# Splitting each tile's second products into two steps, laid between the steps of the next block's first products, in a Fourier-layer and mixture-of-experts kernel

## Chip, cores and metric

The kernel runs on one core of one Trainium2 chip. The metric is the device time of one execution in microseconds (us). The profile has its own execution, with a time and a span (first to last instruction) of its own.

## What is computed

The input is x, 8 batches of 2496 tokens by 256 features, in fp32. A Fourier layer comes first, a mixture of experts after it.

```python
X = rfft(x, axis=1)                       # per batch
Yr = Xr @ w_r - Xi @ w_i + b_r            # 256 x 256
Yi = Xr @ w_i + Xi @ w_r + b_i
Y  = soft_threshold(Yr, Yi, 0.01)
y  = irfft(Y)                             # 19968 tokens x 256
e  = argmax(y @ w_gate)                   # one of 8 experts per token
g  = softmax(y @ w_gate)[e] * sigmoid(y @ w_output_gate)[e]
out = g * (relu(y @ w1[e]) @ w2[e])       # w1: 256 x 1024, w2: 1024 x 256
```

## The kernel before

**Two parts.** The Fourier part works batch by batch: first transform, spectrum, soft threshold, inverse transform; it writes y to DRAM (`yd`). The expert part gathers tokens that are sorted by expert into 163 tiles of 128 tokens. The first 64 tiles hold tokens of the first four batches and are taken as 32 **pairs** (two tiles of one expert, m = 2); the other 99 are **singles** (m = 1), from all batches. A pair or a single is a **block**. The pairs begin while the last batch's inverse is still being computed.

**One block.** A token tile is gathered (`yg`, line 1236, on POOL), scaled and split into two fp16 parts (`yhl`, lines 1255 and 1256, on ACT and DVE) and transposed by a DMA from SP (`eT`, line 1269). The *first products* (`up`, line 1354) multiply it with the first half of the expert's weights, in steps: a single has 2 steps of 24 matmuls of 128 columns, a pair 4 steps of 12 matmuls of 256 columns. Every step has a PSUM bank of its own, which ACT (line 1364) and DVE (line 1365) then read: relu, and a split into two fp16 parts, into `hh`. The *second products* (`down`, line 1325) take 24 matmuls of 256 columns for each tile, from `hh` and the second half of the weights, into one bank. ACT scales the sum into `o` (line 1336), and POOL scatters it to DRAM by an indirect DMA (line 1339).

**Weights.** An expert has 2 MB, kept in DRAM (`wd`) and fetched by SP in two halves of 1 MB: the *up half* and the *down half* (`fetch`, line 1222). There are three buffers (`wbuf`), used in turn; the first four blocks have two of them. A block whose buffer already holds its expert skips its fetch on the device (`cond`). So a new expert costs six halves: two for each of the first three of its blocks. An up half may be loaded when the first products of the block three before (two before, for the first ones) have been read, a down half when that block's second products have.

**What sets the order.** The class `Issue` runs all stages as coroutines over modelled times and writes down each engine's instructions in the order that results; on the chip every engine keeps its order, and waits for semaphores. A request such as `yield "P", r, 2.61, f, True` asks for the engine (P is TensorE, A ACT, D DVE, G POOL, S SP) with a priority `r` (the smallest that is ready goes first), a modelled duration, and a PSUM bank if the last field is there. `r` grows by 5.6 from tile to tile. There are eight PSUM banks, two `hh` places for a pair (each becomes two for singles), three `eT` places for a pair (likewise six for singles) and five of `yhl`. The second products are asked for by `block` when all steps of `hh` have been written (`io.set("hh", t)`), with the priority r + 4m.

Of the kernel before, what the change touches and what calls it, by code (L numbers as in the profile page):

```python
# [15 lines left out]
AF = mybir.ActivationFunctionType  # L16
# [7 lines left out]
N = B * S  # L24
# [93 lines left out]
P = 69.05  # L118
# [21 lines left out]

EARLY = dict(yg=3, yhl=2, eT=1, hh=1, o=1)
PLACES = dict(yg=6, yhl=5, eT=3, hh=2, o=5)
KW = 4
YR, ZR, AN, WR, SR = 2, 3, 6, 3, 6
S1 = 5
# [34 lines left out]
class Issue:  # L180
# [64 lines left out]
    def give(self, slots, n=1):  # L245
        for _ in range(n):
            if slots.queue:
                self.go(slots.queue.pop(0))
            else:
                slots.n += 1  # L250
# [25 lines left out]
def tile_fft_moe(ctx, tc, x, w_r, w_i, b_r, b_i, w_gate, w_og, w1, w2, f1, f4, cmat, gmat, m16, out, dbg=None):  # L276
    nc = tc.nc
    V, A, G, T = nc.vector, nc.scalar, nc.gpsimd, nc.tensor
# [19 lines left out]
    def bank(i):  # L298
        return pps.tile([128, 512], F32, tag=f"ps{i}", name=f"ps{i}")
# [123 lines left out]
    io = Issue(list(range(8)))  # L423
# [4 lines left out]
    st = {}  # L428
# [567 lines left out]
    def plan(ph):  # L996
# [30 lines left out]
        if ph == 0:  # L1027
            route["fl"] = pc.tile([1, T_ALL], I32, name="flg")
            route["ei"] = pc.tile([1, T_ALL], I32, name="ebi")
            V.memset(route["fl"][:, 0:2 * KW + 1], 1)  # L1030
        V.tensor_copy(route["ei"][:, t0:t0 + n], ev[0:1])
        fl = lambda a, b, c, d, step: V.tensor_tensor(route["fl"][:, a:b], eb[0:1, a:b], eb[0:1, c:d:step], ALU.not_equal)
        if ph == 0:
            fl(4, 2 * KW, 0, 2 * KW - 4, 1)
            fl(2 * KW + 1, T_A, 2 * KW - 5, T_A - 6, 1)
        else:
# [38 lines left out]
    sidx = pc.tile([128, T_ALL], I32, name="sidx")  # L1075
# [110 lines left out]
    def open_h():  # L1186
# [5 lines left out]
        io.set("opened")  # L1192
        for k, n in PLACES.items():
            for i in range(EARLY[k], n):
                io.put(slots[k], i)

    def place(k, i, shape, dt):
        return pools["w" if i < EARLY[k] else "h"].tile(shape, dt, tag=f"{k}{i}", name=f"{k}{i}")

    def wplace(k):  # L1200
        return k % 2 if k < KW else (k - KW + 2) % 3

    def before(k):

        return None if k < 2 or k == KW else k - 2 if k < KW else k - 3

    def fetch(r):

        yield "w open"
        for k, (t, n) in enumerate(BLOCKS):  # L1210
            yield "plan", 0 if t < T_A else 1
            if k == KW:
                yield "opened"
# [63 lines left out]
    def part(k, i, shape):  # L1277

        if (k, i) not in parts_:
            parts_[k, i] = place(k, i, shape, F16)  # L1280
        return parts_[k, i]

    def back(k, t, i):

        if t >= T_A:
            io.put(slots[k + "1"], i)
            return
        st["n" + k] = st.get("n" + k, 0) + 1
        if st["n" + k] <= T_A // 2 - PLACES[k]:
            io.put(slots[k], i)  # L1290
        else:
            for h in range(2):
                io.put(slots[k + "1"], (i, h))

    def block(k, r):

        t, m = BLOCKS[k]
        for i in range(m):
            yield "eT", t + i
        ie, eT = st["eT", t]  # L1300
        yield "w", t, 0
        if m == 2:
            ih = yield slots["hh"]
            hh = part("hh", ih, [128, 4096])
        else:
            ih = yield slots["hh1"]
            hh = part("hh", ih[0], [128, 4096])[:, 2048 * ih[1]:2048 * (ih[1] + 1)]
        hh = hh.rearrange("p (v f n) -> p v f n", v=2, f=8)
        w = W[wplace(k)][:, :4096].rearrange("p (c h v f) -> p c h v f", c=2, h=2, v=2)
        st["nh", t], st["nu", t] = 0, 0  # L1310
        for half in range(2 * m):
            io.go(up(t, m, half, w, eT, ie, hh, r))
        yield "hh", t
        yield "w", t, 1
        w = W[wplace(k)][:, 4096:].rearrange("p (i v c d) -> p i v c d", i=4, v=2, c=2)
        for i in range(m):
            io.go(down(t + i, m, i, w, hh, ih, r + 4 * m))

    def down(t, m, n, w, hh, ih, r):
        def f(i):  # L1320
            pt = bank(i)
            k = 0
            for fc in range(8):
                for v, vw in ((0, 0), (0, 1), (1, 0)):
                    T.matmul(pt[:, :256], hh[:, v, fc, 128 * n:128 * n + 128], w[:, fc // 2, vw, fc % 2], start=(k == 0), stop=(k == 23))  # L1325
                    k += 1
            return pt

        i, pt = yield "P", r, 2.61, f, True
        if n == m - 1:  # L1330
            back("hh", t, ih)
            io.set("down", t - n)
        io_ = yield slots["o"]
        o = place("o", io_, [128, 256], F32)
        fac = st.pop(("fac", t))
        yield "A", r - 4, 0.47, lambda: A.activation(o, pt[:, :256], AF.Copy, scale=fac)  # L1336
        io.free(i)
        give("fac")
        yield "G", r - 4, 1.0, lambda: G.indirect_dma_start(out=out, out_offset=bass.IndirectOffsetOnAxis(ap=sidx[:, t:t + 1], axis=0), in_=o, in_offset=None, bounds_check=N - 1, oob_is_err=False)  # L1339
        yield 3.6  # L1340
        io.put(slots["o"], io_)

    def up(t, m, half, w, eT, ie, hh, r):

        c = 4 // m

        def f(i):
            pt = bank(i)
            for j in range(c):
                g = c * half + j  # L1350
                n = 0
                for dh in range(2):
                    for vw, v in ((0, 0), (0, 1), (1, 0)):
                        T.matmul(pt[:, 128 * m * j:128 * m * (j + 1)], w[:, dh, g // 4, vw, 128 * (g % 4):128 * (g % 4) + 128], eT[:, :m, v, dh], start=(n == 0), stop=(n == 5))  # L1354
                        n += 1
            return pt

        i, pt = yield "P", r, (1.34, 1.31)[m - 1], f, True
        st["nu", t] += 1
        if st["nu", t] == 2 * m:  # L1360
            back("eT", t, ie)
            io.set("up", t)
        hv = hh[:, :, c * half:c * half + c].rearrange("p v c n -> p v (c n)")
        yield "A", r, 0.6, lambda: A.activation(hv[:, 0], pt, AF.Relu)  # L1364
        yield "D", r, 0.69, lambda: V.scalar_tensor_tensor(hv[:, 1], pt, 0.0, hv[:, 0], ALU.max, ALU.subtract)  # L1365
        io.free(i)
        st["nh", t] += 1
        if st["nh", t] == 2 * m:
            io.set("hh", t)

    def blocks_(r):
        for k, (t, m) in enumerate(BLOCKS):
            yield "w open"
            io.go(block(k, r + 5.6 * t))
# [47 lines left out]
```

## Time and profile before

| | before |
|---|---|
| time, median of 3 runs | 1507.56 us (1501.02 to 1515.1) |
| profiled execution | 1500.14 us; span 1498.4 us |
| busy TensorE, matmuls / weight loads | 1420.1 / 1280.4 us (95% / 85%) |
| busy DVE, ACT, POOL | 970.0, 717.4, 590.9 us |
| mean granted TensorE clock | 0.983 |
| DMA | 285.33 MB, mean 190 GB/s |

Busy times are sums over an engine's instructions. Matmuls are pipelined and their ends are modelled, so how fast TensorE goes is read from the starts of its rows and from the gaps before them. A row of the timeline gives start, length, engine, line, operation, tiles and count; the brackets at its end hold the idle time before it and what ended it. The rows of waits give engine, line and what was waited for, then the sum in us, how often, and the longest. The rows of windows give for a stretch the busy time of each engine with instructions in brackets, the granted clock, the DMA share and GB/s.

### The profile page before, as it was taken

What the parts mean: (1) busy time and instruction counts of PE and PEld (TensorE: products, weight loads), DVE (VectorE), ACT (ScalarE), POOL (GpSimd) and SP (SyncE); (2) the same over time, 40 slices, a digit from 0 to 9 for tenths busy, and PEclk for the clock granted to TensorE, in tenths of its full rate; (3) what the DMA queues carried; (4) which work ended last, traced back from release to release, by engine and by line L of the source; (5) the groups of instructions that cost most, each with busy time, mean ns of one, the idle gap of its engine ahead of it and who ended that gap; (6) DMA issues with size and microseconds to landing.
All of it is one profiled execution on the core that took longest, in us unless ns stands there. A gap on an engine that the chain in (4) does not pass through costs nothing. (4 is left out here: it accounts for less than half of the span.)

```text
span 1498.4 us, 42257 instructions
## 1 busy us (share of the span) xinstructions
PE 1420.1 (95%) x16192; PEld 1280.4 (85%) x16192; DVE 970.0 (65%) x2911; ACT 717.4 (48%) x1386; POOL 590.9 (39%) x664
## 2 busy tenths in 40 slices
PE   4799999998989989999999999999999999999998
PEld 4689887887778867878999988999898989999997
DVE  3677777769988878677777685555454555454532
ACT  4666765767665746343333333433333333333432
POOL 0454535444455545334333324344243333433311
PEclk8799999999999999999999999999999999999999
DMA  8879999999989898988865788765938476477420
GB/s 227 198 164 212 217 225 198 218 221 214 215 209 209 205 223 202 208 241 231 239 185 147 213 227 218 220 208 123 233 80 234 106 208 220 98 235 212 102 51 20
DMA packets 329955, 285.33 MB, mean 190 GB/s; under 512 B 277702, under 2 KB 286536, under 8 KB 317721
## 3 DMA queue, kind: packets, MB, share of 16 engines
q1 hardware_dynamic: 313127, 239.40, 65.4%
q0 software_dynamic: 15648, 42.17, 10.5%
q8 instruction: 127, 2.08, 0.6%
q10 hardware_dynamic: 978, 1.06, 0.3%
q14 instruction: 75, 0.61, 0.1%
HBM read 337.41 MB, written 58.91 MB: 264 GB/s over the span
## 5 line engine op out<-in xcount | busy, mean ns | idle before, releaser
L1354 PE MATMUL ps<-eT,wbuf 128*128 128x128 f16 (+1 forms) x6288 | 451.9, 232 | 5.6 <-DMA wbuf<-wd 4.3
L1325 PE MATMUL ps<-wbuf,hh 128*128 128x256 f16 x3912 | 444.8, 273 | 8.9 <-DVE hh L1365 4.0
L1354 PEld LDWEIGHTS <-wbuf 128*128 128x128 f16 x6288 | 419.7, 98 | 26.0 <-DMA wbuf<-wd 5.2
L1325 PEld LDWEIGHTS <-hh 128*128 128x128 f16 x3912 | 379.5, 98 | 57.0 <-DVE hh L1365 6.5
L1339 POOL DMA_INDIRECT out<-o,sidx x163 | 167.4, 1027 | 494.0 <-ACT o L1336 270.7
L1365 DVE SCALAR_TENSOR_TENSOR hh<-ps,hh 128x512 f16<-128x512 f32 x326 | 220.3, 689 | 206.7 <-ACT hh L1364 195.3
L1364 ACT ACTIVATE hh<-ps 128x512 f16<-128x512 f32 x326 | 188.3, 596 | 194.1 <-PE ps L1354 176.7
L670 PE MATMUL ps<-whl,xt 128*128 128x256 f16 x1920 | 229.3, 276 | 3.8 <-ACT xt L655 1.7
L670 PEld LDWEIGHTS <-xt 128*128 128x128 f16 x1920 | 190.2, 99 | 40.8 <-ACT xt L655 2.5
L1236 POOL DMA_INDIRECT yg<-yd,gidx x163 | 161.2, 989 | 93.2 <-DVE p2e L366 35.4
L1256 DVE SCALAR_TENSOR_TENSOR yhl<-yg,ys,yhl 128x256 f16<-128x256 f32 x163 | 79.6, 488 | 145.1 <-ACT yhl L1255 135.6
L1336 ACT ACTIVATE o<-ps,fac 128x256 f32<-128x256 f32 x163 | 76.8, 471 | 200.0 <-PE ps L1325 168.4
L1255 ACT ACTIVATE yhl<-yg,ys 128x256 f16<-128x256 f32 x163 | 82.2, 505 | 160.6 <-DMA eT<-yhl 78.1
L588 PE MATMUL ps<-f1t,x 117*128 117x120 f32 (+1 forms) x704 | 91.3, 291 | 6.1 <-issue 4.9
L588 PEld LDWEIGHTS ps<-f1t,x 117*128 117x128 f32 (+1 forms) x704 | 88.7, 207 | 7.4 <-issue 5.0
L689 POOL CAST zhl<-z 128x512 f16<-128x512 f32 x44 | 28.4, 647 | 139.1 <-DVE z L686 70.8
L765 PE MATMUL ps<-bdt,f4t 120*117 120x512 f16 x264 | 70.4, 390 | 10.5 <-ACT ste L716 8.5
L700 PE MATMUL ps<-gt,zhl 128*128 128x128 f16 x960 | 65.3, 220 | 9.9 <-DVE zhl L690 3.9
L700 PEld LDWEIGHTS <-zhl 128*128 128x128 f16 x960 | 58.1, 98 | 17.4 <-DVE zhl L690 4.4
L597 ACT ACTIVATE at<-ps,sx 128x480 f16<-128x480 f32 (+1 forms) x88 | 55.3, 649 | 34.2 <-PE ps L588 31.5
L685 ACT ACTIVATE zhl<-ps,sc 128x512 f32<-128x512 f32 x80 | 54.7, 687 | 32.9 <-PE ps L670 28.2
L690 POOL TENSOR_TENSOR zhl<-z,zhl 128x512 f16<-128x512 f32 x51 | 60.6, 1188 | 24.8 <-ACT zhl L688 21.4
(187 smaller groups left out, 1610.5 us busy)
## 6 DMA issues: line engine op xcount, KB each, us to landing
wbuf<-wd SPq DMA_DIRECT2D x262, 1024.0 KB
yd<-yt SPq DMA_DIRECT2D x120, 158.4 KB
x<-in_x SPq DMA_DIRECT2D x120, 156.0 KB
wr<-in_moe_w SPq DMA_DIRECT2D x32, 512.0 KB
wd<-wsp SPq DMA_DIRECT2D x64, 256.0 KB
yg<-yd,gidx POOLq DMA_INDIRECT x163
eT<-yhl SPq DMA_TRANSPOSE x163
out<-o,sidx POOLq DMA_INDIRECT x163
```

Source lines behind the costliest of these rows:

```text
L588: T.matmul(pv[:, dh, :, m * j:m * j + m], xs[:k, j0 + j, 128 * dh:128 * dh + 128], fw, start=True, stop=True)
L670: T.matmul(yp[:, 256 * j:256 * j + 256], xt_[:, v, 2 * dh + j, 64 - 64 * u:192 - 64 * u], whl[:, dh, vw, 256 * u:256 * u + 256], start=Fal ...
L700: T.matmul(bv[:, j], zhl[:, vz, c:c + 128], gt[:, 2 * p + j, v], start=(n == 0), stop=(n == 2))
L1236: yield "G", r + 5.6 * t - 30, 1.0, lambda: G.indirect_dma_start(out=yg, out_offset=None, in_=src, in_offset=bass.IndirectOffsetOnAxis(ap= ...
L1255: yield "A", r - 10, 0.5, lambda: A.activation(yhl[:, 0], yg[:, :256], AF.Copy, scale=s)
L1256: yield "D", r - 10, 0.48, lambda: V.scalar_tensor_tensor(yhl[:, 1], yg[:, :256], s, yhl[:, 0], ALU.mult, ALU.subtract)
L1325: T.matmul(pt[:, :256], hh[:, v, fc, 128 * n:128 * n + 128], w[:, fc // 2, vw, fc % 2], start=(k == 0), stop=(k == 23))
L1336: yield "A", r - 4, 0.47, lambda: A.activation(o, pt[:, :256], AF.Copy, scale=fac)
L1339: yield "G", r - 4, 1.0, lambda: G.indirect_dma_start(out=out, out_offset=bass.IndirectOffsetOnAxis(ap=sidx[:, t:t + 1], axis=0), in_=o, i ...
L1354: T.matmul(pt[:, 128 * m * j:128 * m * (j + 1)], w[:, dh, g // 4, vw, 128 * (g % 4):128 * (g % 4) + 128], eT[:, :m, v, dh], start=(n == 0) ...
L1364: yield "A", r, 0.6, lambda: A.activation(hv[:, 0], pt, AF.Relu)
L1365: yield "D", r, 0.69, lambda: V.scalar_tensor_tensor(hv[:, 1], pt, 0.0, hv[:, 0], ALU.max, ALU.subtract)
```

## The change

A tile's second products become two steps of 12 matmuls into the same bank; the bank is given back after the second. The first takes the first half of `hh` and may start when that is written (for a single, one step of first products; for a pair, two); the second waits for the rest. The priorities are set so that the steps of a block's second products alternate with the steps of the next block's first products: the steps of first products are now 2.8 apart (before, all had the same priority), and the second products stand at r + 5.6m + 1.4 and on, by 2.8. No matmul is added or left out. The line numbers of the new kernel are one higher for the fetch and the transposes; first products are line 1364, second products 1329, `hh` lines 1374 and 1375, `o` 1346 and the scatter 1349.

```diff
+UP, DN = 2.8, 1.4
...
         for half in range(2 * m):
-            io.go(up(t, m, half, w, eT, ie, hh, r))
-        yield "hh", t
-        yield "w", t, 1
+            io.go(up(t, m, half, w, eT, ie, hh, r + UP * half))
         w = W[wplace(k)][:, 4096:].rearrange("p (i v c d) -> p i v c d", i=4, v=2, c=2)
         for i in range(m):
-            io.go(down(t + i, m, i, w, hh, ih, r + 4 * m))
+            io.go(down(t + i, m, i, w, hh, ih, r + (5.6 + UP * i) * m + DN))
 
     def down(t, m, n, w, hh, ih, r):
-        def f(i):
-            pt = bank(i)
+        t0 = t - n
+        yield "w", t0, 1
+        def f(i=None):
+            if half == 0:
+                st["pt", t] = i, bank(i)
             k = 0
-            for fc in range(8):
+            for fc in range(4 * half, 4 * half + 4):
                 for v, vw in ((0, 0), (0, 1), (1, 0)):
-                    T.matmul(pt[:, :256], ..., start=(k == 0), stop=(k == 23))
+                    T.matmul(st["pt", t][1][:, :256], ..., start=(half == k == 0), stop=(half == 1 and k == 11))
                     k += 1
-        i, pt = yield "P", r, 2.61, f, True
+        for half in range(2):
+            for i in range(m * half, m * half + m):
+                yield "hh", t0, i
+            if half == 0:
+                yield "P", r, 1.31, f, True
+            else:
+                yield "P", r + UP, 1.31, f
+        i, pt = st.pop(("pt", t))
...
-        yield "A", r - 4, 0.47, lambda: A.activation(o, ...)
+        yield "A", r - DN, 0.47, lambda: A.activation(o, ...)
...
-        st["nh", t] += 1
-        if st["nh", t] == 2 * m:
-            io.set("hh", t)
+        io.set("hh", t, half)
```

The order of ACT mirrors that of TensorE, since each step of first products is followed by one write of `hh` and each tile's second products by one `o`. Among the singles, ACT before:

```order
L1336 ACTIVATE o4_22336<-ps4_22243,fac6_21011 128x256
L1364 ACTIVATE hh1_9602<-ps5_22310 128x512
L1364 ACTIVATE hh1_9602<-ps3_22343 128x512
L1364 ACTIVATE hh0_9453<-ps2_22372 128x512
L1364 ACTIVATE hh0_9453<-ps6_22418 128x512
L1336 ACTIVATE o0_22512<-ps7_22446,fac7_21072 128x256
L1255 ACTIVATE yhl1_22476<-yg0_21820,ys0_22482 128x256
L1255 ACTIVATE yhl2_22537<-yg1_21880,ys1_22547 128x256
L1336 ACTIVATE o1_22580<-ps0_22487,fac8_21255 128x256
```

ACT at the same place now:

```order
L1346 ACTIVATE o4_22394<-ps3_22297,fac6_20970 128x256
L1374 ACTIVATE hh0_9453<-ps7_22369 128x512
L1256 ACTIVATE yhl1_22435<-yg0_21757,ys0_22467 128x256
L1374 ACTIVATE hh0_9453<-ps6_22438 128x512
L1346 ACTIVATE o0_22516<-ps0_22419,fac7_21092 128x256
L1374 ACTIVATE hh0_9453<-ps4_22491 128x512
L1256 ACTIVATE yhl2_22557<-yg1_21879,ys1_22589 128x256
L1374 ACTIVATE hh0_9453<-ps1_22560 128x512
L1346 ACTIVATE o1_22638<-ps2_22541,fac8_21214 128x256
```

Before, four writes of `hh` (two singles) stood together, and then two results `o` with two splits `yhl` between them; now there is one `o` and one `yhl` for every two writes of `hh`, in turn.

SP in the same stretch, its register loads left out; the fetches of `wbuf` are those of three consecutive singles, up half and down half, before:

```order
L1269 DMA_TRANSPOSE eT2_9495<-yhl1_23025 128x4x128 [waits DMAHW7_49,DVE_49]
L1269 DMA_TRANSPOSE eT0_9316<-yhl2_23208 128x4x128 [waits DMAHW0_49,DVE_49,PE_49]
L1222 DMA wbuf1_8931<-wd_79 128x4096 [waits DMAHW1_49,PE_49]
L1222 DMA wbuf2_9195<-wd_79 128x4096 [waits DMAHW2_49]
L1222 DMA wbuf2_9195<-wd_79 128x4096 [waits DMAHW3_49,PE_49]
L1222 DMA wbuf0_8930<-wd_79 128x4096 [waits DMAHW4_49,PE_49]
L1269 DMA_TRANSPOSE eT0_9316<-yhl3_23269 128x4x128 [waits DMAHW5_49,DVE_49]
```

SP at that place now, in the same way:

```order
L1223 DMA wbuf1_8931<-wd_79 128x4096 [waits DMAHW7_49]
L1270 DMA_TRANSPOSE eT0_9316<-yhl2_23167 128x4x128 [waits DMAHW0_49,DVE_49,PE_49]
L1223 DMA wbuf1_8931<-wd_79 128x4096 [waits DMAHW1_49,PE_49]
L1223 DMA wbuf2_9195<-wd_79 128x4096 [waits DMAHW2_49]
L1270 DMA_TRANSPOSE eT0_9316<-yhl3_23289 128x4x128 [waits DMAHW3_49,DVE_49,PE_49]
L1223 DMA wbuf2_9195<-wd_79 128x4096 [waits DMAHW4_49,PE_49]
L1223 DMA wbuf0_8930<-wd_79 128x4096 [waits DMAHW5_49]
```

Two transposes stood together after every second single's up half; now one stands between the up half and the down half of every single, and each of them waits for TensorE.

More of the change, by code (lines that the diff above doesn't have):

```diff
@@ L1309, in block @@
         w = W[wplace(k)][:, :4096].rearrange("p (c h v f) -> p c h v f", c=2, h=2, v=2)
-        st["nh", t], st["nu", t] = 0, 0
+        st["nu", t] = 0
         for half in range(2 * m):
-            io.go(up(t, m, half, w, eT, ie, hh, r))
-        yield "hh", t
-        yield "w", t, 1
+            io.go(up(t, m, half, w, eT, ie, hh, r + UP * half))
         w = W[wplace(k)][:, 4096:].rearrange("p (i v c d) -> p i v c d", i=4, v=2, c=2)
         for i in range(m):
-            io.go(down(t + i, m, i, w, hh, ih, r + 4 * m))
+            io.go(down(t + i, m, i, w, hh, ih, r + (5.6 + UP * i) * m + DN))
     def down(t, m, n, w, hh, ih, r):
-        def f(i):
-            pt = bank(i)
+        t0 = t - n
[3 more added lines that the diff above has]
+                st["pt", t] = i, bank(i)
             k = 0
-            for fc in range(8):
+            for fc in range(4 * half, 4 * half + 4):
                 for v, vw in ((0, 0), (0, 1), (1, 0)):
-                    T.matmul(pt[:, :256], hh[:, v, fc, 128 * n:128 * n + 128], w[:, fc // 2, vw, fc % 2], start=(k == 0), stop=(k == 23))
+                    T.matmul(st["pt", t][1][:, :256], hh[:, v, fc, 128 * n:128 * n + 128], w[:, fc // 2, vw, fc % 2], start=(half == k == 0), stop=(half == 1 and k == 11))
                     k += 1
-            return pt
-        i, pt = yield "P", r, 2.61, f, True
+        for half in range(2):
[6 more added lines that the diff above has]
+        i, pt = st.pop(("pt", t))
         if n == m - 1:
-            back("hh", t, ih)
-            io.set("down", t - n)
+            back("hh", t0, ih)
+            io.set("down", t0)
         io_ = yield slots["o"]
@@ L1335, in down @@
         fac = st.pop(("fac", t))
-        yield "A", r - 4, 0.47, lambda: A.activation(o, pt[:, :256], AF.Copy, scale=fac)
+        yield "A", r - DN, 0.47, lambda: A.activation(o, pt[:, :256], AF.Copy, scale=fac)
         io.free(i)
         give("fac")
-        yield "G", r - 4, 1.0, lambda: G.indirect_dma_start(out=out, out_offset=bass.IndirectOffsetOnAxis(ap=sidx[:, t:t + 1], axis=0), in_=o, in_offset=None, bounds_check=N - 1, oob_is_err=False)
+        yield "G", r - DN, 1.0, lambda: G.indirect_dma_start(out=out, out_offset=bass.IndirectOffsetOnAxis(ap=sidx[:, t:t + 1], axis=0), in_=o, in_offset=None, bounds_check=N - 1, oob_is_err=False)
         yield 3.6
```

## The prediction

> **What bounds the kernel now.** First the page's busy times, to see which engine can be the limit; then the windows over the expert part, for what TensorE leaves idle there; then the waits, for what that idle time is made of.
>
> ```profile
> span 1498.4 us, 42257 instructions
> PE 1420.1 (95%) x16192; PEld 1280.4 (85%) x16192; DVE 970.0 (65%) x2911; ACT 717.4 (48%) x1386; POOL 590.9 (39%) x664
> ```
>
> ```profile
> 600.00:1450.00 850.00, 836.25 (x9823) 769.15 (x9822) 505.08 (x1694) 319.60 (x622) 304.99 (x307) 1.00 0.69 186
> 1400.00:1450.00 50.00, 50.00 (x670) 47.30 (x668) 23.26 (x68) 18.64 (x35) 10.92 (x11) 1.00 0.26 60
> 400.00:450.00 50.00, 43.70 (x411) 37.24 (x410) 43.03 (x104) 33.28 (x66) 20.41 (x27) 0.93 0.94 213
> ```
>
> TensorE is the bound: from 600 to 1450 us it is idle for 850 - 836.25 = 13.75 us, at full clock. The change moves no instruction of the earlier stages ahead of its first second-product step, and leaves the number of matmuls alone. So what can be won is these 13.75 us, 0.9% of the span. The waits from 600 to the end name 13.2 of them:
>
> ```profile
> PE ps L1354 <- DMA wbuf<-wd: 4.3, 4, 1.4
> PE ps L1325 <- DVE hh L1365: 4.0, 9, 1.0
> PE ps L1325 <- ACT hh L1364: 3.1, 5, 0.9
> PE ps L1325 <- issue: 1.2, 2, 0.8
> PE ps L1325 <- PE ps L1354: 0.4, 1, 0.4
> PE ps L1354 <- issue: 0.2, 1, 0.2
> ```
>
> Two kinds: first products that wait for a new expert's weights (4.3 and 0.2, so 4.5 us), and second products that wait for `hh` or the like (8.7 us). Where do they lie? Without a new expert, singles run like this:
>
> ```profile
> 1448.65 5.52 PE L1354 MATMUL ps<-eT,wbuf 128*128 128x128 f16 x96
> 1454.01 5.40 PE L1325 MATMUL ps<-wbuf,hh 128*128 128x256 f16 x48
> 1459.25 5.52 PE L1354 MATMUL ps<-eT,wbuf 128*128 128x128 f16 x96
> ```
>
> Two singles' first products (96), then their second products (48), in 1459.25 - 1448.65 = 10.60 us without a gap. Around a new expert (there are seven among the later singles) it looks so:
>
> ```profile
> 1061.39 5.40 PE L1325 MATMUL ps<-wbuf,hh 128*128 128x256 f16 x48
> ...
> 1077.23 2.84 PE L1354 MATMUL ps<-eT,wbuf 128*128 128x128 f16 x48
> 1081.34 2.85 PE L1354 MATMUL ps<-eT,wbuf 128*128 128x128 f16 x48 [1.27 <-DMA wbuf<-wd]
> 1084.61 0.39 PE L1325 MATMUL ps<-wbuf,hh 128*128 128x256 f16 x2 [0.41 <-PE ps L1354]
> 1085.33 5.20 PE L1325 MATMUL ps<-wbuf,hh 128*128 128x256 f16 x46 [0.33 <-DVE hh L1365]
> ```
>
> A wait for weights in the middle of the 96, then two short waits ahead of the second products. Call the first single of the new expert k. The half that comes too late is the up half of k+2.
>
> **The change, part by part.**
>
> *Switching between first and second products.* Every single now switches four times instead of once on average, and a pair some four times more often: about 300 + 130 = 430 more switches. Does one cost anything? A row's length holds the modelled time of its last matmul:
>
> ```profile
> L1325 PE MATMUL ps<-wbuf,hh 128*128 128x256 f16 x240 | 27.0, 273 | 0.0
> L1354 PE MATMUL ps<-eT,wbuf 128*128 128x128 f16 x430 | 25.0, 219 | 0.0
> ```
>
> 5.52 - 0.22 = 5.30 us are 95 distances of 55.8 ns; from the last start to the first second product are 5.36 - 5.30 = 0.06, one more such distance. The other way 5.40 - 0.27 = 5.13 are 47 distances of 109 ns, and 5.24 - 5.13 = 0.11 is one more. So a switch costs 0, within the rows' 0.01 us: 0 in the sum, 4 us either way in the range.
>
> *The weights of k+2.* All down halves and up halves pass through SP in order, and through the DMA queue behind each other. The chain starts at A, the end of the second products of k-3, which frees the place of k's down half: A = 1061.39 + 2.62 = 1064.01 here (half of the 48). The first products of k+2 are due at 1077.23 + 48 x 0.0558 = 1079.91, 15.9 us after A. They come at 1081.34: four halves (k down, k+1 up and down, k+2 up) and the transposes among them take 17.3 us to be usable. The stretches show why that is not shorter:
>
> ```profile
> 1063.00:1067.00 4.00, 4.00 (x42) 3.62 (x41) 1.37 (x7) 0.47 (x1) 1.02 (x1) 1.00 1.50 152
> 1067.00:1070.00 3.00, 3.00 (x58) 3.00 (x56) 1.39 (x7) 1.30 (x4) 0.97 (x1) 1.00 1.06 373
> 1070.00:1073.00 3.00, 3.00 (x49) 2.90 (x47) 2.24 (x5) 2.13 (x5) 0.60 (x1) 1.00 1.05 430
> ```
>
> Three us after A move little (152 GB/s; two transposes run there), then a half of 1.05 MB takes 2.5 to 2.8 us. Now the new order: from A to the first step of k+2 stand twelve steps, six of first products (24 x 55.8 ns = 1.34) and six of second (12 x 109 ns = 1.31), which is again 15.9 us. And between A and that half there are still two transposes on SP. So I expect the same lateness, but at every new expert. Before, it depended on the parity of k. Where k+2 stands first in its 96, two whole periods, 21.2 us, lie between, and nothing waits:
>
> ```profile
> 1275.70 5.52 PE L1354 MATMUL ps<-eT,wbuf 128*128 128x128 f16 x96
> ```
>
> ```profile
> 1340.89 4.29 PE L1354 MATMUL ps<-eT,wbuf 128*128 128x128 f16 x74
> ```
>
> The other four are:
>
> ```profile
> 1011.91 5.71 PE L1354 MATMUL ps<-eT,wbuf 128*128 128x128 f16 x96
> ```
>
> ```profile
> 1147.33 2.85 PE L1354 MATMUL ps<-eT,wbuf 128*128 128x128 f16 x48 [1.12 <-DMA wbuf<-wd]
> ```
>
> ```profile
> 1213.62 2.85 PE L1354 MATMUL ps<-eT,wbuf 128*128 128x128 f16 x48 [1.44 <-DMA wbuf<-wd]
> ```
>
> ```profile
> 1386.60 2.85 PE L1354 MATMUL ps<-eT,wbuf 128*128 128x128 f16 x48 [0.47 <-DMA wbuf<-wd]
> ```
>
> Five waits of 0.2 (5.71 against 5.52), 1.27, 1.12, 1.44 and 0.47 us, mean 0.9. Seven of these are 6.3 us instead of 4.5: **1.8 us lost**. Ends: none left (4.5 won), or seven of the longest, 10.1 (5.6 lost).
>
> *The waits of the second products.* Of the 8.7 us, 5.5 stand at six of the seven new experts, as in 0.41 and 0.33 above. ACT explains them:
>
> ```profile
> 1074.81 0.47 ACT L1336 ACTIVATE o<-ps,fac 128x256 f32<-128x256 f32 x1 [1.96 <-issue]
> 1081.64 0.51 ACT L1255 ACTIVATE yhl<-yg,ys 128x256 f16<-128x256 f32 x1 [6.36 <-DMA eT<-yhl]
> 1083.96 2.05 ACT L1364 ACTIVATE hh<-ps 128x512 f16<-128x512 f32 x4
> ```
>
> A split `yhl` waits 6.36 us for a transpose that is queued behind the weights, and behind it on ACT stand four writes of `hh`, which the second products need. How much delay do these bear? In the steady state the last DVE write ends as follows:
>
> ```profile
> 1454.90 0.69 DVE L1365 SCALAR_TENSOR_TENSOR hh<-ps,hh 128x512 f16<-128x512 f32 x1 [0.65 <-ACT hh L1364]
> ```
>
> That is 1455.59, 1.6 us after the first products ended (1453.95), and the second tile's products start at 1454.01 + 2.62 = 1456.63: 1.0 us to spare. Now four steps, 2 x 1.34 + 2 x 1.31 = 5.3 us, lie between a step and the second products that read it: 3.7 us to spare. A transpose also has fewer halves ahead of it, since it is issued between them. I leave 1.5 us of the 5.5: **4.0 us won**. Ends: nothing and 5.5.
>
> *The beginning,* where pairs run beside the last inverse:
>
> ```profile
> 656.37 0.60 ACT L769 ACTIVATE yt<-ps 117x512 f32<-117x512 f32 x1 [3.59 <-DMA yd<-yt]
> ```
>
> ```profile
> PE ps L1325 <- DVE hh L1365: 2.0, 3, 1.0
> PE ps L1325 <- issue: 0.4, 1, 0.4
> ```
>
> ACT waits 3.59 us for a store to `yd`, and second products wait 2.4 us (650 to 700). For pairs the new order has at least five steps of 1.31 between, 6.5 us instead of 2.6, so this wait should shrink; but the inverse's steps move some 8 us forward among TensorE's work, and their stores press closer. I take 1.0 left: **1.4 us won**. Ends: 2.4 won, and 3 lost (another such wait of ACT).
>
> *Left at nothing:* 0.8 us of `issue` with no shown cause stays. A pair's `hh` place and down half are held longer, by some 4 us; but a down half still has two pair blocks, over 20 us, and a half takes under 3 us of the queue. The scatters on POOL come evenly; POOL is 39% busy, and TensorE does not wait for it.
>
> **Sum:** -1.8 + 4.0 + 1.4 = 3.6 us. The profiled execution of 1500.14 us becomes 1496.5. The median of the runs, 1507.56, stands 0.5% above that execution; on its scale 1496.5 x 1.005 = **1504 us**, 0.2% faster. The expected gain is small, since one wait is made rarer and another is made regular.
>
> **The rivals.**
>
> *All waits go.* If the transposes, now apart, leave the queue free for k's down half right after A (the 152 GB/s stretch), then 1.4 us come earlier than before, and the mean lateness of 0.9 is gone, with 5.5 and 2.4: 12.4 us, 1487.7, or 1495 on the median's scale. Against it: one transpose still stands right ahead of k's down half. 17%.
>
> *Slower: transposes between the halves.* Each transpose now waits for TensorE on SP, with the down half and the next up half queued behind it, and one runs between k+1's two halves, ahead of k+2's up half. SP spends about 1.2 us on one:
>
> ```profile
> 1069.94 7.80 SPq L1269 DMA_TRANSPOSE eT<-yhl  x2
> 1082.29 3.51 SPq L1269 DMA_TRANSPOSE eT<-yhl  x2
> ```
>
> (3.51 for two with a wait between; 7.80 where the queue was full.) If 1.2 us comes on top of 0.9 at all seven, the loss is 7 x 2.1 - 4.5 = 10.2, less 5.4: 1505, on the median's scale 1512. It decides when the transposes among the four halves cost more than the two before A do now. If k+1's up half, due eight steps (10.6 us) after A, is late by as much, another 7 x 1.2 = 8.4: 1521. Its chain is 3.0 + 2 x 2.6 = 8.2 us, plus 1.2, so there is some room. 18% and 4%.
>
> *The clock.* The granted clock is 1.00 through the expert part, and 0.93 in a stretch with more gaps (400 to 450). If short gaps at the many switches cost it, 900 us at 0.93 are 68 us more: 1568, or 1576. Nothing in the rows speaks for it, since a switch shows no gap. 2%. [...]
>
> *Nothing changes,* because ACT is held as long as before and the waits only change place: 1500, or 1507.6. 9%.
>
> **Chances and range.** My forecast 50%, and the rivals 17, 22, 2 and 9. About 1% is what a measurement of this kernel can tell from no change. No case but the clock and the double lateness passes 1% by itself; the first rival (0.8%) with 4 us of switches in its favour does, as does the second with 4 us against it: faster 0.11, same 0.78, slower 0.11. The range goes from below the first rival to above the second: 1489 to 1515.
>
> **What would show it.** Right: rows of first and second products of 24 and 12 in turn without gaps; waits for `wbuf` at about seven new experts, of about 1 us; waits of line 1329 for `hh` below 3 us; the clock at 1.00. Wrong: gaps at switches; two waits for weights at each new expert; TensorE waiting for `eT`; long waits in the first 100 us of the pairs.

## The result, and the profile after

The changed kernel is **slower by 0.76%**: 1519.43 us in the median of its 16 runs (1510.23 to 1526.9) against 1508.12 us of the kernel before (16 runs, 1501.02 to 1515.56), ratio 1.0076 (95% interval 1.005 to 1.0101). The forecast was 1504, with a range of 1489 to 1515. Its profiled execution took 1517.81 us, 17.7 more than the one of before, so the traces show somewhat more of the loss than the medians (11.3 us) do.

The page's busy times:

```profile
span 1516.0 us, 42073 instructions
PE 1428.7 (94%) x16192; PEld 1286.7 (85%) x16192; DVE 967.5 (64%) x2911; ACT 720.2 (48%) x1386; POOL 589.7 (39%) x664
```

TensorE is idle for 1516.0 - 1428.7 = 87.3 us (78.3 before, 9.0 more) and busy for 8.6 us more with the same 16192 matmuls. Together these are the span's 17.6 us, so there are two losses to find. The waits of TensorE from 600 us to the end hold the first:

```profile
PE ps L1364 <- DMA wbuf<-wd: 19.7, 12, 3.0
PE ps L1364 <- issue: 4.0, 5, 1.8
PE ps L1329 <- issue: 0.9, 1, 0.9
```

Second products (now line 1329) no longer wait for `hh` at all; the 8.7 us of before are gone, those of the beginning with them. In their place stand 19.7 us in which first products (line 1364) wait for weights; there were 4.5. The windows over the same part, and the four 50 us stretches with the lowest clock, hold the second loss:

```profile
600.00:1500.00 900.00, 874.63 (x10278) 804.80 (x10277) 511.23 (x1707) 332.01 (x641) 309.44 (x313) 0.99 0.63 178
900.00:950.00 50.00, 46.26 (x405) 40.23 (x404) 25.39 (x84) 17.62 (x34) 24.43 (x25) 0.97 0.72 232
1000.00:1050.00 50.00, 46.45 (x606) 43.12 (x604) 23.60 (x78) 17.85 (x34) 15.96 (x16) 0.97 0.72 190
1200.00:1250.00 50.00, 47.93 (x632) 44.66 (x629) 23.69 (x75) 17.05 (x34) 17.91 (x18) 0.97 0.68 196
1400.00:1450.00 50.00, 46.98 (x615) 43.81 (x613) 24.14 (x75) 19.14 (x36) 13.93 (x14) 0.97 0.40 94
1022.60:1026.00 3.40, 3.40 (x26) 2.78 (x23) 2.59 (x8) 1.82 (x4) 0.97 (x1) 0.50 1.08 305
```

From 600 us on TensorE is idle for 900 - 874.63 = 25.4 us instead of 13.75. The clock column (third from the end) was 1.00 in this part before. Now four stretches have 0.97, and the last row shows what lies in one of them: 3.4 us at 0.50. Four such episodes cost about 4 x 1.7 = 6.8 us. Of the 8.6 us 2.5 lie ahead of 600 us (545.21 us busy there instead of 542.67), so the episodes account for the other 6.1.

Where the weights come late is seen in TensorE's timeline at one new expert, the same one that the prediction looks at:

```profile
1071.29 1.50 PE L1364 MATMUL ps<-eT,wbuf 128*128 128x128 f16 x24
...
1083.66 1.51 PE L1364 MATMUL ps<-eT,wbuf 128*128 128x128 f16 x24 [1.61 <-DMA wbuf<-wd]
1085.01 1.47 PE L1329 MATMUL ps<-wbuf,hh 128*128 128x256 f16 x12
1086.32 1.50 PE L1364 MATMUL ps<-eT,wbuf 128*128 128x128 f16 x24
1087.66 1.47 PE L1329 MATMUL ps<-wbuf,hh 128*128 128x256 f16 x12
1090.11 1.51 PE L1364 MATMUL ps<-eT,wbuf 128*128 128x128 f16 x24 [0.97 <-DMA wbuf<-wd]
```

Steps of 24 and 12 follow each other without gaps (1085.01 + 1.31 = 1086.32, 1086.32 + 1.34 = 1087.66). The first row begins where the second products of k-3 end: 1071.29 is A. Twelve steps, 15.9 us, after A the first products of k+2 are due, and eight steps, 10.6 us, after A those of k+1. These come at 1083.66, 12.4 us after A, and wait 1.61 us; those of k+2 come 18.8 us after A. **Two waits at one new expert**, where the prediction had one. The twelve waits are seven at k+2 (0.97 to 3.02 us, 15.7 in all) and five at k+1 (0.29 to 1.61 us, 4.05 in all).

Why the halves take so long is seen in SP's issues after A, and in the windows over the same time:

```profile
1070.17 1.23 SPq L1270 DMA_TRANSPOSE eT<-yhl  x1
1072.08 2.18 SPq L1223 DMA_DIRECT2D wbuf<-wd  x2
1075.47 1.55 SPq L1270 DMA_TRANSPOSE eT<-yhl  x1
1077.38 2.53 SPq L1223 DMA_DIRECT2D wbuf<-wd  x2
1080.77 1.27 SPq L1270 DMA_TRANSPOSE eT<-yhl  x1
```

```profile
1073.00:1076.00 3.00, 3.00 (x42) 2.83 (x40) 1.82 (x7) 1.46 (x3) 0.28 (x2) 1.00 0.96 265
1076.00:1079.50 3.50, 3.50 (x48) 3.29 (x47) 1.70 (x4) 1.20 (x3) 0.95 (x1) 1.00 1.02 356
1079.50:1083.50 4.00, 2.55 (x35) 2.15 (x32) 0.66 (x6) 0.00 (x0) 1.02 (x1) 1.00 1.10 158
1083.50:1089.00 5.50, 5.34 (x72) 4.95 (x72) 2.75 (x9) 1.84 (x4) 0.97 (x1) 1.00 0.96 388
```

At 1072.08 k's down half and k+1's up half are issued; at 1075.47 a transpose, which waits for TensorE; at 1077.38 k+1's down half and k+2's up half. The transpose between k+1's two halves costs SP 1.55 us, but the core's DMAs move only 158 GB/s (last column) for 4 us, 1079.5 to 1083.5, against 356 and 388 around it, with the DMA engines busy (1.10, the column before). It is not SP that holds the halves there, since it has issued k+1's down half and k+2's up half by 1077.38 + 2.53 = 1079.91. k+1's first products begin only as the stretch ends, at 1083.66.

The trace's DMA packets show one transpose, 512 packets of 256 bytes, spread over this stretch. It is a long case: at the seven new experts a transpose among the halves takes 0.5 to 4.2 us. Packets of POOL's indirect DMAs lie in the stretch too, with 59.8% of the 16 engines' time (48.4% for SP's queue). They are not needed for it: from 1146.6 to 1149.0, with 4.5% for POOL's packets, another transpose passes (2.4 us) while the DMAs move 130 GB/s, and 368 in the 3 us behind it. That the transpose is the cause is so far only suggested by these rows; the experiments test it.

### The profile page after: what moved, and what is told of

It is laid out like the page before. It is cut to its first block, busy times and chain, and to the rows that moved or that the text cites. A ratio compares the mean times of both kernels' runs of the same rounds, so it can differ in the third digit from the quotient of the medians.

```text
span 1516.0 us, 42073 instructions
## 1 busy us (share of the span) xinstructions
PE 1428.7 (94%) x16192; PEld 1286.7 (85%) x16192; DVE 967.5 (64%) x2911; ACT 720.2 (48%) x1386; POOL 589.7 (39%) x664
## 3 DMA queue, kind: packets, MB, share of 16 engines
q0 software_dynamic: 15648, 42.17, 10.1%
## 5 line engine op out<-in xcount | busy, mean ns | idle before, releaser
L1364 PE MATMUL ps<-eT,wbuf 128*128 128x128 f16 (+1 forms) x6288 | 486.4, 233 | 23.9 <-DMA wbuf<-wd 19.7
L1329 PE MATMUL ps<-wbuf,hh 128*128 128x256 f16 x3912 | 480.3, 274 | 0.9 <-issue 0.9
L1364 PEld LDWEIGHTS <-wbuf 128*128 128x128 f16 x6288 | 432.7, 98 | 50.6 <-DMA wbuf<-wd 23.4
L1375 DVE SCALAR_TENSOR_TENSOR hh<-ps,hh 128x512 f16<-128x512 f32 x326 | 225.1, 690 | 274.4 <-ACT hh L1374 236.2
L1374 ACT ACTIVATE hh<-ps 128x512 f16<-128x512 f32 x326 | 193.7, 594 | 294.9 <-PE ps L1364 267.2
L1256 ACT ACTIVATE yhl<-yg,ys 128x256 f16<-128x256 f32 x163 | 82.2, 505 | 186.9 <-DMA eT<-yhl 98.7
```

Source lines behind the costliest of these rows:

```text
L1256: yield "A", r - 10, 0.5, lambda: A.activation(yhl[:, 0], yg[:, :256], AF.Copy, scale=s)
L1329: T.matmul(st["pt", t][1][:, :256], hh[:, v, fc, 128 * n:128 * n + 128], w[:, fc // 2, vw, fc % 2], start=(half == k == 0), stop=(half == ...
```

## The experiments

Twelve kernels ran on three occasions, each on another chip, on which the kernel before took 1513.64, 1510.16 and 1501.34 us. So absolute times are not compared across them; each ratio is to the kernel before of the same occasion, with its 95% interval in brackets. The theories: **weights** (the whole loss stands at the seven new experts), **queue** (a transposing DMA between two halves holds up the queue by 3 to 4 us, however short its issue), **waiting on SP** (what counts is that each transpose waits for TensorE, with the halves behind it) and **deadline** (even spacing alone moves the due time of k+1 and k+2 too close).

**Without the new experts among the later singles.** Both orders, once with the fetches of the later new experts skipped:

```diff
-fl(T_A + 3, T_ALL, T_A, T_ALL - 3, 1)
+V.memset(route["fl"][:, T_A + 3:T_ALL], 0)
```

> The kernel before, with the weights of the singles not reloaded after the first three of them (the later experts' weights are left out, so wrong experts are applied there). Theory 'weights': all of the loss of the change arises at the seven new experts. Then here the waits for wbuf (4.5 us) and the waits of second products behind them (5.5 us) go: about 10 us below the kernel before, 1498. Rival 'elsewhere': no new information from this one alone; also about 1498.

> The changed kernel, with the weights of the singles not reloaded after the first three of them (the later experts' weights are left out). Theory 'weights': the changed kernel loses its 20 us of waits for wbuf and is at or below the same variant of the kernel before, about 1494 to 1498. Rival 'elsewhere' (switches, the beginning, the clock by itself): it stays 8 to 11 us above that variant, about 1507.

Measured: 1499.18 us, 0.9911 (0.9876 to 0.9946) with the old order, and 1497.16 us, 0.9877 (0.9813 to 0.994) with the new one. The intervals overlap, and the new order's median is the lower one. The loss lies at the new experts: without them there is none, and the new order's TensorE shows no wait for weights there. What its TensorE waits for most from 600 us on is

```profile
PE ps L1329 <- issue: 3.5, 7, 0.9
```

**Where the transposes stand and what they wait for.** The old order of TensorE with transposes forced apart, as in the new one; and the new order of TensorE with the transposes forced into pairs on SP, as in the old one (`io.set("f", t, m)` marks each half as issued):

```diff
+        if t >= T_A + 8:
+            yield "f", t - 3, 0                          # x_before: one transpose per block
+            yield "f", t - 3 + (t - T_A + 1) % 2, 0      # x_after: two, after every second up half
```

> The kernel before, its TensorE order untouched, with the singles' transposes placed on SP as in the changed kernel: one after every single's up half instead of two after every second. Theory 'queue' (a transpose between two halves holds up the weights' DMA queue by 3 to 4 us): waits for wbuf rise from 4.3 to 10 us or more, time up by 5 to 10 us. Rival 'waiting on SP' (the halves are late since the transposes ahead of them wait for TensorE): here they need no such wait, so no change. Rival 'deadline' (the even spacing of the blocks alone makes the halves late): no change, 4.3 us.

> The changed kernel, its TensorE order untouched, with the singles' transposes placed on SP as in the kernel before: two after every second single's up half, none after the other. Theory 'queue': where the two stand ahead of the first half, the waits become about 1 us; where they stand in the middle, they stay or grow; in sum 19.7 falls to 10 to 14. Rival 'waiting on SP': the transposes no longer wait for TensorE here, so the waits fall to 6 or less. Rival 'deadline': still about 20 us.

Measured: x_before 1513.99 us, 1.0012 (0.9988 to 1.0037), so no change; x_after 1514.85 us, 1.0015 (0.9987 to 1.0042). The waits of TensorE in x_before from 600 us on, then ACT's row at one late transpose:

```profile
PE ps L1328 <- ACT hh L1367: 7.7, 5, 2.5
PE ps L1357 <- DMA wbuf<-wd: 4.1, 3, 1.7
PE ps L1328 <- DVE hh L1368: 4.0, 10, 1.0
```

```profile
1353.52 0.51 ACT L1256 ACTIVATE yhl<-yg,ys 128x256 f16<-128x256 f32 x1 [6.00 <-DMA eT<-yhl]
```

My expectation of longer waits for weights missed. They stayed at 4.1 us; instead the transposes themselves came late behind the halves, ACT stood 6.00 us at a `yhl`, and the writes of `hh` behind it held the second products. The old order has 1.0 us of room there, so the run doesn't isolate what the transposes do to the weights. x_after does so in part:

```profile
PE ps L1367 <- DMA wbuf<-wd: 10.4, 8, 3.5
```

With the transposes in pairs again the waits for weights fall from 19.7 to 10.4 us, within the 10 to 14 that "queue" gave. They don't fall to the 6 or less that "waiting on SP" gave, though in this kernel a transpose hardly waits for TensorE when its turn comes (from 900 to 1480 us 28.8 us in 6 waits, against 226.7 in 97 in the changed kernel).

**Plain copies for the transposes.** The same order and the same waits on SP, with every transposing DMA replaced by a plain one of the same bytes, in the new order and in the old:

```diff
-nc.sync.dma_start(eT.rearrange("p v c n -> p (v c) n"), yhl.rearrange("p v d -> p (v d)"), transpose=True)
+nc.sync.dma_start(eT.rearrange("p v c n -> p (v c n)"), yhl.rearrange("p v d -> p (v d)"))
```

> The changed kernel, with a plain copy of the same 128 KB in the place of each transposing DMA on SP, with its waits (the transposition of the token tiles is left out). Theory 'queue' (a transposing DMA between two halves holds the weights' queue): waits for wbuf fall from 19.7 to 6 us or less, and the time to the kernel before's or some 5 us below. Rival 'waiting on SP' and rival 'deadline': the order and waits on SP are as in the changed kernel, so 15 to 20 us of waits stay.

> The kernel before, with a plain copy of the same 128 KB in the place of each transposing DMA (the transposition of the token tiles is left out). It gives the changed kernel with plain copies (0.9918 of the kernel before) its measure: what the new order of TensorE is worth when the weights' queue is free. Theory 'queue': both orders keep hardly a wait for wbuf; the old order keeps some waits for hh, so 0.992 to 0.997 here. Rival (the new order itself is worse, and the plain copies help by some other way): 0.985 or less here.

Measured: p_after 1497.63 us, 0.9918 (0.9885 to 0.9952), and p_before 1486.58 us, 0.9911 (0.9878 to 0.9943) on a later occasion. The waits of p_after, its SP at a copy, and the windows where the new order's 4 us had been:

```profile
PE ps L1329 <- issue: 3.8, 6, 1.1
PE ps L1364 <- DMA wbuf<-wd: 1.6, 4, 0.8
```

```profile
1074.90 0.49 SPq L1270 DMA_DIRECT2D eT<-yhl  x1
```

```profile
1068.00:1090.00 22.00, 21.76 (x299) 20.41 (x297) 11.96 (x38) 8.09 (x16) 7.20 (x8) 1.00 0.90 351
```

This is the run that decides. The order, the deadlines and SP's waits for TensorE are those of the changed kernel (the copies wait 218.9 us in 96 waits where the transposes waited 226.7 in 97); only the kind of DMA differs. The waits for weights fall from 19.7 to 1.6 us, the DMAs move 351 GB/s over these 22 us (293 in the changed kernel over the same ones), and the two orders gain as much (0.9918 and 0.9911; for p_before I had given 0.992 to 0.997). So neither the deadline nor the waiting on SP makes the loss without the transposing DMA: of the theories **queue** stands, in so far as it names the transposing DMA. One reservation: SP issues a plain copy faster too (0.49 us instead of 1.23 to 1.55). For the two transposes among the halves that is 1.5 to 2.1 us at an expert, less than the (19.7 - 1.6) / 7 = 2.6 that were won. How much of those 2.6 is SP's and how much the queue's is not separated by this run. For the queue speaks the stretch of 158 GB/s, in which SP had already issued the halves.

**The transposes on ACT's queue.** If the loss is the place in SP's queue, another queue might cure it; for the later singles:

```diff
-yield from move(r - 10, 1.4e5, 1.2, lambda: nc.sync.dma_start(..., transpose=True))
+yield "A", r - 10, 0.1, lambda: nc.scalar.dma_start(..., transpose=True)
```

> The changed kernel, with the singles' transposing DMAs issued from ACT, so through another DMA queue. Theory 'queue': the weights no longer stand behind the transposes in their queue; waits for wbuf fall to 8 us or less, time at or below the kernel before (1495 to 1505). Rival 'waiting on SP': the same fall. Rival 'deadline': 15 to 20 us stay. A risk for all: ACT waits for each transpose's source and spends time on issuing, so writes of hh come later; with 3.7 us to spare I expect no waits of second products from that.

> The kernel before, with the singles' transposing DMAs issued from ACT. Theory 'queue': its waits for wbuf (4.3) fall to about 1 us, and with them the splits that ACT waits for; time down by up to 5 us, unless ACT's issuing delays the writes of hh, for which this order has only 1.0 us to spare: then waits of line 1325 for hh grow. Rival 'deadline': 4.3 us stay.

Measured: 1568.15 us, 1.04 (1.0351 to 1.0449), and with the old order 1.0346 (1.0252 to 1.0441): far worse, and not expected. The waits of t_after, ACT at one place, and the windows there:

```profile
PE ps L1332 <- ACT hh L1377: 26.2, 11, 7.3
PE ps L1367 <- DMA wbuf<-wd: 19.8, 9, 4.2
```

```profile
1102.85 0.51 ACT L1256 ACTIVATE yhl<-yg,ys 128x256 f16<-128x256 f32 x1 [13.03 <-DMA eT<-yhl]
```

```profile
1085.00:1090.50 5.50, 5.50 (x79) 5.23 (x77) 3.13 (x10) 2.17 (x4) 0.98 (x1) 1.00 1.01 347
1090.50:1099.50 9.00, 5.28 (x60) 4.88 (x58) 0.04 (x1) 0.00 (x0) 1.02 (x1) 0.78 1.11 168
```

Beside transposes on another queue the DMAs fall to 168 GB/s for 9 us, and the transpose itself keeps ACT waiting for 13 us. The waits for weights stay at 19.8 us, where "queue" gave 8 or less. So the place in SP's queue is not what counts by itself: from two queues, too, transposes and loads were slow beside each other, with the DMA engines busy (1.11) over these 9 us. POOL's indirect DMAs have 51.7% of the DMA time in these 9 us; what part they have in it is not separated here.

**Singles alone.** The new order and the two steps only for singles, pairs as before:

```diff
+    def new(m):
+        return m == 1
```

> The new order for the singles alone; the pairs keep the order and the whole second products of the kernel before. If the loss is all at the later new experts (theory 'weights'), this kernel loses the same 0.7 to 0.8% as the changed kernel, with about 20 us of waits for wbuf; and 2 to 3 us of waits for hh in the beginning come back. If the pairs' part of the change carries some of the loss, it stands nearer to the kernel before.

Measured: 1521.15 us, 1.0101 (1.0065 to 1.0136), not below the changed kernel's 1.0076, and the intervals overlap. There is no sign that the pairs carry any of the loss; most of the waits for weights are there without them (15.8 us of 19.7):

```profile
PE ps L1370 <- DMA wbuf<-wd: 15.8, 9, 3.5
```

**Another order of the halves.** An up half is free as soon as the first products three blocks back are read, and in the new order k+1's up half is due before k's down half. So for singles each up half goes ahead of the down half of the block before; ux_after also puts the transposes into pairs:

```diff
-        for k, (t, n) in enumerate(BLOCKS):
-            for m in range(2):                  # up k, down k, up k+1, down k+1 ...
+        for k, m in seq:                        # singles: up k+1, down k, up k+2, down k+1 ...
```

> The changed kernel with another order of the singles' fetches: the up half of the next block goes ahead of a block's down half. A half and a transpose less stand ahead of the late up half of k+2, that is 3 us of transfer and up to 4 of the transpose. Theory 'queue': waits for wbuf fall from 19.7 to 4 us or less, time 1495 to 1505, below the kernel before. Rival: the down halves are late in their turn (line 1329 waits for wbuf), and the time stays near the changed kernel's 1519.

> Both at once: up halves ahead, and the singles' transposes in twos behind every second down half. Theory 'queue': one stop of the queue for two transposes instead of two, so at least as good as the up halves ahead alone, waits for wbuf of 0 to 3 us, 1493 to 1503. If two transposes in a row stop the queue for twice as long, it is no better than that, or worse.

> The kernel before with the up halves ahead. Its waits for wbuf (4.3 us) should go; the waits for hh that come from late transposes stay or shrink: 0.995 to 1.0 of the kernel before. If it comes out as low as the changed kernel with up halves ahead, then the gain is the order of the fetches and not that of the matmuls.

Measured: u_after **1482.52 us, 0.9875 (0.9839 to 0.9912)**, faster than both kernels; ux_after 1495.12 us, 0.9974 (0.9945 to 1.0003); u_before 1503.55 us, 1.0023 (0.9993 to 1.0052). The waits of u_after from 600 us on, and its window:

```profile
PE ps L1332 <- DVE hh L1378: 0.7, 1, 0.7
PE ps L1332 <- DMA wbuf<-wd: 0.2, 1, 0.2
```

```profile
600.00:1470.00 870.00, 867.32 (x10299) 803.45 (x10297) 515.40 (x1713) 329.74 (x644) 309.54 (x315) 1.00 0.67 184
```

TensorE is idle for 2.7 us of 870, at full clock. The transposing DMAs still stand between the halves; what is new is what stands ahead of each half. With it SP's waits for TensorE moved from the transposes (20.8 us in 4 waits from 900 to 1480 us, 226.7 in 97 in the changed kernel) to the fetches, so this run is a cure and not a second proof of the cause. k+1's up half now has none of the others between itself and A (it had k's down half), and k+2's has two (it had three), while k's down half is due only 11.9 us after A. The gain needs both parts. With the old order of TensorE (u_before) second products wait for `hh` for 8.6 us and for weights for 3.9: the waits for weights, which I had expected to go, only moved to them. With the transposes in pairs (ux_after), which I had expected to be at least as good, ACT waits longer for the transposes (99.9 us from 600 us on, 75.6 in u_after), and second products wait again. u_before, then ux_after:

```profile
PE ps L1328 <- ACT hh L1367: 4.6, 4, 2.2
PE ps L1328 <- DVE hh L1368: 4.0, 9, 1.0
PE ps L1328 <- DMA wbuf<-wd: 3.9, 2, 2.6
```

```profile
PE ps L1335 <- ACT hh L1380: 6.4, 7, 1.6
PE ps L1335 <- DVE hh L1381: 5.9, 10, 0.7
```

## Why the prediction was wrong

*What could be won:* right in kind. u_after, which is left with 2.7 us of TensorE's idle time, has a span 12.5 us below that of before. Its gain by the medians, 18.8 us (13.2 to 24.2), lies above the 13.75 that I set as the limit, though the interval reaches it; so the size is not confirmed.

*Switches cost nothing:* right. There is no gap between the steps, and u_after runs 870 us at 1.00 with the same switching. The rival of the clock therefore didn't come about in the form that I gave it.

*The waits of the second products:* right in sign, too careful in size. I left 1.5 us of the 5.5 and 1.0 at the beginning; what remains is one wait of 0.9 without a shown cause. The transposes still come late for ACT (98.7 us of such waits from 600 us on, 78.1 before), but no second product waits for `hh`.

*The weights of k+2:* **this step failed.** The due time of 15.9 us after A was right, and so was that all seven experts would wait. The size was not: 6.3 us were forecast, 19.7 came, beyond even the end of 10.1 that I gave the term. The sentence that failed is "between A and that half there are still two transposes on SP. So I expect the same lateness". I counted transposes and priced one by SP's 1.2 us. Before, two in a row stood ahead of k's down half and the stretch behind them had 152 GB/s for 4 us; that row held the price, and I read it as a delay at the start of the chain only. Apart, one alone stood in such a stretch (158 GB/s for 4 us), and one now lies between k+1's up half and its down half. So the term was mis-sized since the places of the transposes among the halves count, and not only their number. p_after shows that it is the kind of DMA that costs this (19.7 us of waits for weights, 1.6 with plain copies).

*The second rival* had the right place, a transpose between k+1's two halves, and priced it too low, by SP's 1.2 us. Its form with k+1's up half late too, which I priced at 1521 and gave 4%, is nearest to what was measured (five of the seven experts wait at k+1). That 1521 is so near 1519 is partly luck: it had 7 x 2.1 + 8.4 = 23.1 us of waits for weights (19.7 came) and neither the half clock nor the `issue` waits. I thought k+1 had "some room", by a chain of 8.2 us and 1.2; the chain took 12.4.

*Not in the sum at all:* the half clock. TensorE's timeline behind a long wait:

```profile
1021.92 2.19 PE L1364 MATMUL ps<-eT,wbuf 128*128 128x128 f16 x24 [2.98 <-DMA wbuf<-wd]
1023.91 2.49 PE L1329 MATMUL ps<-wbuf,hh 128*128 128x256 f16 x12
1026.23 1.50 PE L1364 MATMUL ps<-eT,wbuf 128*128 128x128 f16 x24
```

A step of 24 takes 1023.91 - 1021.92 = 1.99 us and the next of 12 takes 2.32, instead of 1.34 and 1.31: 1.7 us lost behind a wait of 2.98. The trace's records of the granted clock have 3.413 us at 0.50 for each of the four episodes, which begin at 920.16, 1022.56, 1223.95 and 1404.86 us: 30, 59 and 53 times 3.413 us apart. All other changes of the clock in these records, from the start of the span on, lie on the same grid, wherever the waits begin. With that grid it fits that the longer of two waits was the harmless one here. After these waits

```profile
1157.35 1.51 PE L1364 MATMUL ps<-eT,wbuf 128*128 128x128 f16 x24 [3.01 <-DMA wbuf<-wd]
1223.37 2.25 PE L1364 MATMUL ps<-eT,wbuf 128*128 128x128 f16 x24 [2.07 <-DMA wbuf<-wd]
```

the one of 3.01 us is followed at full rate (1.51 for a row) and the one of 2.07 is not (2.25). An edge of the grid, at 1155.68 us, cuts the first into 1.34 and 1.67 us; the second lies within one cell (the time between two edges). But a cell need not be all idle: those ahead of the four episodes hold 2.30, 2.77, 2.07 and 2.28 us of idle time, and the most from 600 to 1500 us without an episode behind it is 1.89. So in this part of the trace about 2 us of idle time in one cell were enough. That is no exact limit: ahead of 600 us the same trace has an episode (408.17 to 414.99) behind a cell with 1.25.

By the terms of the sum, from 600 us on: weights 19.7 - 4.5 = 15.2 us lost, second products 8.7 - 0.9 = 7.8 won (the beginning included), and 4.0 lost in waits of first products named `issue`. That is 11.4 us; the windows have 25.37 - 13.75 = 11.6. The half clock adds 6.8. The `issue` waits stay open. Most of them lie between 914 and 919 us, and the trace names nothing that they wait for. They may not belong to the change: all traces of the first two occasions have such waits in the expert part, the old order's too (n_before 5.9 us), and the four traces of the third have none. They also precede one of the four episodes of half clock, so about 1.7 of the 6.8 us hang on them and not on the weights. Ahead of 600 us, of which the change touches only the last 8, the new execution was idle for 2.5 us less and busy for as much more, which adds nothing to the loss.

## What to carry to other kernels

Spreading work evenly spreads its deadlines too: before doing so, lay the chain of transfers beside the shortest time that any of them will now have, and check their order by due time (here up halves first, which turned a loss of 0.76% into a gain of 1.25%). Price a transposing DMA between others by what the queue moves while it runs (here 158 GB/s for 4 us), not by the time its issue takes (1.55). A wait of TensorE can cost more than its length: behind one of 2.07 us the granted clock stood at 0.50 for 3.41 us, by my estimate half of that or 1.7 us more; behind one of 3.01 it stayed at 1.00.

## What the runs showed of the hardware

- Transposing DMAs of a 128 x 512 fp16 tile among plain loads of 1 MB in one queue took 0.5 to 4.2 us each; the longest stood in a stretch of 4 us at 158 GB/s between stretches of 356 and 388. With plain copies in their place the DMAs moved 351 GB/s over 22 us, with the transposes 293.
- The same transposes on another queue beside the loads: 168 GB/s for 9 us, and a transpose that kept ACT for 13 us.
- TensorE's granted clock fell to 0.50 for 3.41 us behind some waits, on a grid of 3.413 us: in the changed kernel, from 600 to 1500 us, behind cells of that grid with 2.07 to 2.77 us of idle time, and not behind those with 1.89 or less; ahead of 600 us once, for 6.83 us, behind 1.25.
